# Two cached-attention decode steps on one core: groups of four heads with all their rows, 4 MB loads, and one loop of five equal rounds

## The chip, the cores and the metric

The kernel runs on one core of a Trainium2 chip. The metric is the device time of one execution in microseconds. Next to it stands the span of a profiled execution, from its first to its last instruction, mostly 1.4 to 1.6 us shorter than its time. A ratio is the mean time of one kernel's fast runs over the mean of the other's fast runs of the same rounds, so it is not quite the ratio of the medians that are quoted. A difference within 2% counts as "the same".

## The reference

Two independent decode steps, A and B, with the same shapes: one query token, 32 query heads, 16 key/value heads of 128, a cache of 8192 rows. A looks only at the last 2048 rows, B at all of them.

```python
# x [1,1,576], k_cache, v_cache [1,16,8192,128], wq [576,4096], wo [4096,576], all bf16
W = min(4096, max(256, Sk // 4))                      # 2048, for A
q = (x @ wq).reshape(B, Sq, 32, 128).transpose(0, 2, 1, 3)
k = jnp.repeat(k_cache[:, :, Sk - W:, :], 2, axis=1)  # A; B takes all rows
v = jnp.repeat(v_cache[:, :, Sk - W:, :], 2, axis=1)
p = softmax(einsum("bhqd,bhkd->bhqk", q, k) * Dh ** -0.5)
o = einsum("bhqk,bhkd->bhqd", p, v)
out = o.transpose(0, 2, 1, 3).reshape(B, Sq, 4096) @ wo   # [A's 576, B's 576]
```

Every byte is used once: 84 MB of K and V, 9.4 MB of wq, 9.4 MB of wo. This is a job of loading, and the arithmetic has to keep up.

## The kernel before

A small scheduler records operations and works out the semaphore waits; the large ones are emitted in hardware loops. PE (TensorE) transposes K, ACT (ScalarE) and DVE (VectorE) evict the transposes, PE makes scores, ACT the exponentials, PE multiplies with V. Loads are of 2 MB: a slot holds, in each partition, one run of 64 rows of one head, 16 KB.

```python
    def load_kv(arrs, g, s, slots, name, after=()):
        P = 0 if g == 0 else 1
        i = s if g == 0 else 4 * ((g - 1) % 2) + s
        ch = 128 // G[P] * TS                        # G = [4, 2] heads a slot, TS = 64 rows a partition
        r0 = base[P] + (0 if g == 0 else (g - 1) // 2 * ch)
        def src():
            return arrs[P][0, i * G[P]:(i + 1) * G[P], r0:r0 + ch, :].rearrange("g (p t) d -> p g (t d)", t=TS)
        load(slots[:, s, :], src, [(name, s)], "%s%d" % (name, s), after)

    K_ON = lambda g: g < 5
    V_OF = {1: 0, 3: 1, 4: 2, 5: 3, 6: 4}            # in which round each group's V is used
    # [cut: q, transposes, scores, softmax]
    for g in range(7):
        if g < 5:
            for s in range(NS):
                load_kv(ks, g, s, kslots, "k", ...)
        if g in V_OF:
            for s in range(NS):
                load_kv(vs, V_OF[g], s, vslots, "v")
        # [cut: transposes and scores of group g; every second round the softmax of two groups]
        if g == 6:
            weights(0)
            weights(1)
            combine(0)                               # A's heads, ready for wo
        if g in V_OF:
            for s in range(NS):
                v_slot(V_OF[g], s, 20 + s, g)        # 64 matmuls of 128 columns a slot
            v_keep(V_OF[g])                          # DVE: mask and sum of opsum, 2 x 0.69 us
```

K runs ahead of V: the last twelve K and V loads are all V. At the end comes wo, 32 heads of each step, four matmuls of 144 columns a head; B's share is loaded in pieces of 14, 8, 4, 3, 2 and 1 heads.

```python
    combine(1)                                       # B's heads: DVE scales, PE sums, DVE copies
    for P in range(2):
        for Q, lo, n, view, res, after in wo_loads:
            if Q == P:
                wo_part(P, lo, n, view, res)
        finish_out(P)
```

## Time and profile before

The time is 248.36 us (median of 4 runs, 248.31 to 248.45).

| what | before |
|---|---|
| span of the profile | 247.2 us |
| load queue's packets, share of 16 engines | 98.3% |
| bytes read | 102.76 MB |
| PE busy | 69% |
| first to last load packet (from the trace's packet records) | 1.02 to 244.35 us |
| from the last load packet to the end of the span | 2.8 us |

The page of the kernel before: the span, busy time of PE with its share, the DMA row (busy tenths in 40 equal slices), GB/s in those slices, and the load queue with packets, MB and share.

```profile
span 247.2 us, 7504 instructions
...
PE 169.9 (69%) x3406; PEld 132.4 (54%) x3406; DVE 80.9 (33%) x152; ACT 87.2 (35%) x92; POOL 12.9 (5%) x49
...
DMA  8999999999999999999999999999999999999993
GB/s 316 382 446 420 436 424 424 427 427 435 427 426 424 424 432 422 426 424 427 430 432 430 430 424 438 424 427 424 430 427 432 427 432 430 432 425 423 422 410 143
...
q1 hardware_dynamic: 7936, 102.77, 98.3%
```

The load queue never rests. The busy share of PE is an average and does not show a bound here: PE idles 31% of the span while the queue is busy throughout.

The end of the chain of waits (start, duration, what), before:

```profile
220.41 23.98 DMA vslots<-in_B_wo_dram
244.40 0.04 issue
244.44 0.71 PE ktps L654 x10
...
245.18 0.31 DVE outsb L660
```

The chain waits 24 us for B's wo; only ten matmuls and a copy come after it. PE's own timeline there (start, duration, what, in brackets the idle time before it and what ended it):

```profile
222.70 1.08 PE L565 MATMUL opsum<-vslots,ptm 128*32 128x128 bf16 x64 [1.81 <-PEq L214]
226.65 1.92 PE L638 MATMUL misc<-acc,pick 128*128 128x32 f32 x8 [2.87 <-DVE acc L632]
228.49 1.87 PE L654 MATMUL ktps<-kslots,opj 128*32 128x144 bf16 x56
232.25 2.35 PE L654 MATMUL ktps<-kslots,opj 128*32 128x144 bf16 x72 [1.88 <-DMA kslots<-in_A_wo_dram]
238.49 1.87 PE L654 MATMUL ktps<-kslots,opj 128*32 128x144 bf16 x56 [3.89 <-DMA kslots<-in_B_wo_dram]
241.29 1.15 PE L654 MATMUL ktps<-vslots,opj 128*32 128x144 bf16 x32 [0.93 <-DMA vslots<-in_B_wo_dram]
...
244.44 0.68 PE L654 MATMUL ktps<-vslots,opj 128*32 128x144 bf16 x12 [0.15 <-DMA vslots<-in_B_wo_dram]
```

L565 is the last V slot, L638 B's combine, L654 wo. V and combine are done at 228.5, and from there PE follows its loads: nearly every group of wo waits for a DMA.

### The profile page before, as it was taken

To read this page: it belongs to the slowest core of one execution; us is meant where nothing else is said; L and a number is where in the kernel's file an instruction comes from. 1 tells how busy PE (TensorE), PEld (TensorE's weight loads), DVE (VectorE), ACT (ScalarE), POOL (GpSimd) and SP (SyncE) were. 2 spreads that over 40 slices of the span, in tenths; PEclk is the share of its full clock that TensorE was granted. 3 is DMA by queue.
4 is the path that set the end of the run, shared out by engine and by line. 5 is a ranking of instruction groups with operands and counts; after the bars stand their busy time and mean duration, and the time that the engine had idled before them with its cause. 6 is when DMAs were issued, how large, how long until landed. Compare 5 with 4: busy or idle time off the path is not lost. (4 is left out here: it accounts for less than half of the span.)

```text
span 247.2 us, 7504 instructions
## 1 busy us (share of the span) xinstructions
PE 169.9 (69%) x3406; PEld 132.4 (54%) x3406; DVE 80.9 (33%) x152; ACT 87.2 (35%) x92; POOL 12.9 (5%) x49
## 2 busy tenths in 40 slices
PE   0083689993999479995999628998356344574634
PEld 0041286863786368864878428776244243474522
DVE  0010145463755026554555122556005004204000
ACT  2000057757587017776478104775300000000000
POOL 7501000000000000000000000000000000000000
PEclk9999779997999959999799965999957555578555
DMA  8999999999999999999999999999999999999993
GB/s 316 382 446 420 436 424 424 427 427 435 427 426 424 424 432 422 426 424 427 430 432 430 430 424 438 424 427 424 430 427 432 427 432 430 432 425 423 422 410 143
DMA packets 8235, 102.92 MB, mean 416 GB/s; under 512 B 1184, under 2 KB 1312, under 8 KB 2080
## 3 DMA queue, kind: packets, MB, share of 16 engines
q1 hardware_dynamic: 7936, 102.77, 98.3%
q8 instruction: 8, 0.13, 0.2%
q10 hardware_dynamic: 288, 0.00, 0.1%
q14 instruction: 3, 0.02, 0.0%
HBM read 102.76 MB, written 0.00 MB: 416 GB/s over the span
## 5 line engine op out<-in xcount | busy, mean ns | idle before, releaser
L480 ACT ACTIVATE kt<-ktps 128x1024 bf16<-128x1024 bf16 x80 | 78.0, 1021 | 52.9 <-PE ktps L474 52.9
L474 PEld LDWEIGHTS ktps<-ident,kslots 128*128 128x128 bf16 x1280 | 79.3, 104 | 26.2 <-issue 26.2
L474 PE MATMUL ktps<-ident,kslots 128*128 128x128 bf16 x1280 | 85.6, 230 | 10.7 <-PEq L214 10.7
L483 DVE COPY kt<-ktps 128x1024 bf16<-128x1024 bf16 x80 | 55.2, 691 | 52.8 <-PE ktps L474 52.7
L565 PE MATMUL opsum<-vslots,ptm 128*32 128x128 bf16 x1280 | 27.8, 261 | 26.8 <-PEq L214 22.7
L565 PEld LDWEIGHTS opsum<-vslots,ptm 128*32 128x32 bf16 x1280 | 25.0, 119 | 30.8 <-issue 30.7
L494 PE MATMUL sacc<-kt,qst 128*32 128x512 bf16 x320 | 25.7, 392 | 2.1 <-PEq L214 1.9
L574 DVE TENSOR_TENSOR diag<-opsum,rows 128x512 f32<-128x512 f32 x5 | 3.5, 692 | 54.8 <-PE opsum L565 54.8
L433 PE MATMUL opsum<-vslots,xpad 128*32 128x512 bf16 x64 | 8.1, 487 | 17.2 <-DVE xpad L418 12.7
L607 ACT ACTIVATE stat<-stat 128x1 f32<-128x1 f32 (+1 forms) x2 | 0.6, 294 | 36.7 <-DVE stat L605 36.7
L433 PEld LDWEIGHTS opsum<-vslots,xpad 128*32 128x32 bf16 x64 | 2.2, 117 | 20.0 <-issue 13.7
L465 POOL COPY qst<-qtm 128x64 bf16<-128x64 bf16 x20 | 4.5, 236 | 123.1 <-PE sacc L494 114.5
L654 PE MATMUL ktps<-kslots,opj 128*32 128x144 bf16 x184 | 6.1, 325 | 5.8 <-DMA kslots<-in_B_wo_dram 3.9
L439 ACT ACTIVATE qrow<-opsum 128x512 bf16<-128x512 f32 x2 | 1.2, 597 | 24.9 <-PE misc L433 24.9
L494 PEld LDWEIGHTS sacc<-kt,qst 128*32 128x32 bf16 x320 | 5.2, 94 | 8.7 <-issue 4.8
L531 ACT ACTIVATE psb<-sacc,stat 128x2048 bf16<-128x2048 f32 x3 | 5.9, 1967 | 8.5 <-DVE stat L525 8.5
L654 PEld LDWEIGHTS ktps<-kslots,opj 128*32 128x32 bf16 x184 | 5.2, 145 | 6.4 <-DMA kslots<-in_B_wo_dram 4.2
L433 PE MATMUL misc<-vslots,xpad 128*32 128x512 bf16 x64 | 7.9, 475 | 0.0
L441 DVE CAST qrow<-misc 128x512 bf16<-128x512 f32 x2 | 1.4, 692 | 15.9 <-PE misc L433 15.9
L638 PE MATMUL misc<-acc,pick 128*128 128x32 f32 x16 | 3.8, 404 | 3.6 <-DVE acc L632 2.9
L660 DVE CAST outsb<-ktps 128x144 bf16<-128x144 f32 x2 | 0.6, 308 | 16.1 <-PE ktps L654 16.1
L638 PEld LDWEIGHTS misc<-acc,pick 128*128 128x128 f32 x16 | 3.6, 328 | 3.8 <-DVE acc L632 3.0
(66 smaller groups left out, 62.1 us busy)
## 6 DMA issues: line engine op xcount, KB each, us to landing
kslots<-in_B_k_cache_dram SPq DMA_DIRECT2D x16, 2048.0 KB, 20.1
vslots<-in_B_v_cache_dram SPq DMA_DIRECT2D x16, 2048.0 KB, 18.5
kslots<-in_A_k_cache_dram SPq DMA_DIRECT2D x4, 2048.0 KB, 30.4
vslots<-in_A_v_cache_dram SPq DMA_DIRECT2D x4, 2048.0 KB, 24.1
vslots<-in_A_wq_dram SPq DMA_DIRECT2D x2, 2048.0 KB, 9.9
vslots<-in_B_wq_dram SPq DMA_DIRECT2D x2, 2048.0 KB, 20.3
kslots<-in_A_wo_dram SPq DMA_DIRECT2D x2, 2016.0 KB, 23.8
kslots<-in_B_wo_dram SPq DMA_DIRECT2D x1, 2016.0 KB, 31.2
```

Of the source, the lines that this page charges most:

```text
L433: ins = pe.matmul(qps[c][32 * j:32 * j + 32, :], lhsT=xpad[:, P, x, :], rhs=src[:, o:o + 512], start=(u == 0), stop=(u == WQ_UNITS - 1))
L441: add("dve", lambda dve: dve.tensor_copy(qrow[:, 512:1024], misc[:, :]), reads=[B_M], writes=[("qrow", 1)])
L465: add("pool", lambda pool: pool.tensor_copy(qst[:, s * 64:(s + 1) * 64], qtm[:, o:o + 64]), reads=[("qtm", KIND[g])], writes=[("qst", s)], ...
L474: ins = pe.matmul(ktps_bf[q][:, t * 128:(t + 1) * 128], lhsT=kslots[:, s, o:o + 128], rhs=ident[:, :], start=True, stop=True, is_transpose ...
L480: add("act", lambda act, q=q, dst=dst: act.activation(dst, ktps_bf[q], ACT.Copy), reads=[("bank", q)], writes=[("kt", u % NKT, q)], tag="e ...
L483: add("dve", lambda dve, q=q, dst=dst: dve.tensor_copy(dst, ktps_bf[q]), reads=[("bank", q)], writes=[("kt", u % NKT, q)], tag="e%d%d" % ( ...
L494: ins = pe.matmul(sacc[32 * j:32 * j + 32, 512 * half:512 * half + 512], lhsT=qst[:, s * 64 + e * 32:s * 64 + e * 32 + 32], rhs=rhs, start ...
L531: return act.activation(psb[:, :].rearrange("p (x g) -> p x g", g=2), src, ACT.Exp, bias=st(P, C_NB + k), scale=SCALE, accum_out=st(P, C_L ...
L565: ins = pe.matmul(opsum[32 * j:32 * j + 32, s * DH:(s + 1) * DH], lhsT=ptm[:, o:o + 32], rhs=vslots[:, s, b * 128:(b + 1) * 128], start=(u ...
L574: return dve.tensor_tensor(diag[:, g % 2, :, :], opsum[:, :].rearrange("p (s d) -> p d s", s=NS), m, ALU.mult)
L638: ins = pe.matmul(misc[:, 0:32], lhsT=pick[:, r, :], rhs=acc[:, d, 32 * r:32 * r + 32], start=(r == 0), stop=(r == 3))
L654: ins = pe.matmul(ktps[P][32 * j:32 * j + 32, 0:OUTW], lhsT=opj[:, P, jj:jj + 32], rhs=view[:, o:o + OUTW], start=(jj == 0), stop=(jj == H ...
```

## The change

The intent is longer runs and a simpler loop. Four heads with all 8192 rows make a group, so each partition of a B load holds 128 rows of one head, 32 KB, and a load is 4 MB. A's 2048 rows give 8 KB runs, in loads of 1 MB. A group's scores fit one bank without masking, V is multiplied 512 columns at a time, and every round does the same: K, softmax, V.

```diff
-SLOT = 8192
+SLOT = 16384
 ...
+            if g:
+                i = 4 * (g - 1) + 2 * s
+                return sp.dma_start(dst, arrs[1][0, i:i + 2, :, :].rearrange("e (p t) d -> p e (t d)", t=128))
+            for m in range(4):
+                i = 4 * m + 2 * s
+                src = arrs[0][0, i:i + 2, SK - W_A:, :].rearrange("e (p t) d -> p e (t d)", t=32)
+                ins = sp.dma_start(dst[:, m * UNIT:(m + 1) * UNIT], src)
 ...  [cut: scores of eight heads in one bank, no zeroing, no mask]
-                        ins = pe.matmul(opsum[32 * j:32 * j + 32, s * DH:(s + 1) * DH], lhsT=ptm[:, o:o + 32],
-                                        rhs=vslots[:, s, b * 128:(b + 1) * 128],
+                    ins = pe.matmul(opsum[32 * j:32 * j + 32, s * 512:(s + 1) * 512], lhsT=ptm[:, o:o + 32],
+                                    rhs=v[:, :, b:b + 128], start=(tt == 0), stop=(tt == 7), skip_group_check=True)
 ...
+            m = bass.AP(tensor=maskV, offset=0, ap=[[8, 128], [1, 8], [0, DH]])
+            return dve.tensor_tensor(diag[:, :, :], opsum[:, :].rearrange("p (y d) -> p y d", y=8), m, ALU.mult)
 ...
+    for g in range(NG):                    # five equal rounds
+        for s in range(2):
+            load_kv(ks, g, s, koff(s), KS[s], "k")
+        for s in range(2):
+            load_kv(vs, g, s, voff(s), VS[s], "v")
 ...  [cut: transposes, scores]
+        softmax_exp(g)
+        softmax_transpose(g, 18)
+        if g == NG - 1:
+            weights(g)
+            combine(0, (g, 18.6, LAST))
+        v_slot(g, 0, 20)
+        v_slot(g, 1, 21)
+        v_keep(g)
 ...  wq: one load of 36 KB rows for each step, in place of three of 16, 16 and 4 KB
+        (0, 0, 32, 0, [("k", 0), ("k", 1, 0)]),          # wo: step, first head, heads, place
+        (1, 0, 24, WQ_W, [("k", 1, 1)]),
+        (1, 24, 5, 2 * SLOT, [("v", 0, 0), ("v", 0, 1)]),
+        (1, 29, 2, 2 * SLOT + 5 * DM, [("w", 0)]),
+        (1, 31, 1, 2 * SLOT + 7 * DM, [("w", 1)])]
     combine(1)
     for P in range(2):
         [both wo parts, as before]
```

## The prediction

> **What bounds the kernel now.** The DMA queue, from start to end. The page shows DMA at 9 tenths or more in 38 of 40 slices and the load queue at 98.3% of 16 engines. It moves 102.76 MB, 424 to 432 GB/s in the middle (GB/s row). No compute engine exceeds 69%. The chain of waits ends in 24.0 us of DMA (B's wo), then 0.71 us of PE, a copy and the output store. So only four things move the time: the stream's rate, holes in it, its start, and what follows its last byte.
>
> **Rate.** The trace's DMA packets are one per row of a load: 16384 B takes 611 ns at best, 4096 B 159 ns. That is 8.3 ns fixed plus bytes at 27.2 B/ns, or 435 GB/s over 16 engines: the ceiling that the Trainium skill gives (DMA: Bandwidth & Descriptors, "Where 436 GB/s comes from"); the trace agrees. Estimates from this fit, if a longer row stays one packet: 8 KB 310 ns, 32 KB 1214, 36 KB 1365. Per engine: B's K and V 156.4 -> 155.4 us, A's 39.1 -> 39.6, wq 22.1 -> 21.8, wo 22.5 -> 22.0, fewer completions -0.1. Sum about -1.3 us, all on the critical path.
>
> **Holes in the steady part.** None expected. A round brings 16 MB, about 39 us. Its PE work, by the timeline: 8 units of transposes and scores at 2.5 us warm (3 to 3.6 cold), 20 to 28 us; softmax and transpose about 4; V 4 to 7. K's first slot is free about 11 us after landing, while 20 us of loads are queued behind it. V in 512-column matmuls streams the same columns (1280x128 = 320x512); it saves weight loads. Score zeroing, the mask and two-group chunks go too. All off the path.
>
> **Start.** The x loads share the engines: in the trace each alternates one 10 B x packet with one 16 KB row, as the Trainium skill says (same page, "Queues, rings and completion order": round-robin at packet granularity). x A landed at 11.5 us, x B at 13.7. With 36 KB rows each turn costs 1.36 us: I estimate x A at 16 to 19 us, x B near 25. B's q matmuls then end near 31 to 32 us (before 29.4). They gate A's second K load; the first K load runs out near 33 us. An issue takes about 1 us to its first packet: a hole of 0 to 2 us, expected 0.5.
>
> **End.** wo B's first piece grows from 14 heads to 24. The 14 took 1.87 us of PE, 0.118 us a head at the granted 0.5 clock; 24 take 2.8, then 8 more 0.95, against 2.9 us for the remaining small loads. PE finishes some 0.4 us later after the last byte than before.
>
> **Sum.** 248.4 - 1.3 + 0.5 + 0.4 = **248.0 us**, range 246.3 to 250.0. Faster by over 2%: 0.03. Within 2%: 0.92. Slower: 0.05.
>
> **What would show it.** 32 KB packets near 1214 ns, 8 KB near 310; mean GB/s up by at most 2. In the DMA queue's own waits, the one for the q matmuls ends at 31 to 32 us, and the DMA slice around 32 to 36 us is lower. x lands late. PE runs without a break over its last 128 matmuls. PE's busy share falls.
>
> **What would make it wrong.** Rows over 16 KB split into several packets: no rate gain, but no late x. A larger stride between the engines' addresses slowing HBM reads. A fixed cost at load boundaries that I missed. A starting hole of 3 us or more. Coarser slots starving the queue in a cold-clock round.

## The result

The changed kernel takes 249.76 us (249.68 to 250.01, 4 runs) against 248.36: ratio 1.0058, 95% interval 1.0043 to 1.0072. The median is inside the predicted range (one run, 250.01, is just outside) and inside 2%, but 1.4 us slower where 0.4 faster was expected.

| what | before | after |
|---|---|---|
| time | 248.36 us | 249.76 us |
| span of the profile | 247.17 us | 248.39 us |
| first to last load packet | 1.02 to 244.35 | 1.01 to 242.71 |
| from the last load packet to the end | 2.82 us | 5.69 us |
| packets of K and V, median | 16 KB: 0.614 us | 32 KB: 1.218 us; 8 KB: 0.312 us |

The spans differ by 1.22 us, and this splits, to 0.01 us: the loads end 1.64 us earlier, and what follows them is 2.87 us longer. The page after, the same lines:

```profile
span 248.4 us, 5439 instructions
...
PE 165.4 (67%) x2428; PEld 117.5 (47%) x2428; DVE 87.3 (35%) x140; ACT 87.3 (35%) x95; POOL 10.7 (4%) x48
...
DMA  9998999999999999999999999999999999999980
GB/s 350 410 463 372 421 423 421 420 421 420 446 449 438 433 423 427 422 422 443 434 433 438 433 427 427 427 433 433 433 438 443 422 427 433 422 454 411 433 334 9
...
q1 hardware_dynamic: 5632, 102.77, 97.0%
```

The last slice shows it: the DMA row ends in 0 and the rate in 9 GB/s, where before it was 3 and 143. The loads are done and the kernel is not. (Single slices swing by 20 to 40 GB/s because a packet is counted whole; the 8 KB stretch from slice 5 to 10 at 420 and the 32 KB stretch after it are the readings.) The end of the chain of waits after:

```profile
232.24 1.24 DVE diag L548
233.48 0.02 issue
233.50 1.87 DVE acc L384
235.37 0.79 DVE accs L599 x4
236.16 0.04 issue
236.21 1.19 PE misc L612 x29
237.40 3.40 PE ktps L627 x105
240.80 1.21 issue
242.01 2.18 PE ktps L627 x127
244.19 1.65 issue
245.84 0.55 PE ktps L627 x21
```

No DMA stands in it any more. V ends, DVE keeps its result (1.24 + 1.87 us), scales it, PE combines it (L612), and only then come all 256 wo matmuls (L627) in one row, A's 128 as well. PE's timeline:

```profile
225.85 6.33 PE L540 MATMUL opsum<-slots,ptm 128*32 128x512 bf16 x64
236.21 1.19 PE L612 MATMUL misc<-accs,pickB 128*32 128x32 f32 x29 [4.02 <-DVE accs L599]
...
237.37 3.43 PE L627 MATMUL ktps<-slots,opj 128*32 128x144 bf16 x102
242.01 2.18 PE L627 MATMUL ktps<-slots,opj 128*32 128x144 bf16 x127 [1.21 <-issue]
245.84 0.54 PE L627 MATMUL ktps<-slots,opj 128*32 128x144 bf16 x21 [1.65 <-issue]
```

PE idles 4.02 us for the keep although A's heads were ready at 226.2 and A's wo had landed (its last packet ended at 231.6). B's first 24 heads were in at 239.9 and PE reached B's part only at about 242.4, 20 matmuls after its first pause. Twice PE stops with "issue": nothing that the profile shows held it.

### The profile page after: what moved, and what is told of

Same layout as the page of the kernel before. It is cut to its first block, busy times and chain, and to the rows that moved or that the text cites. A ratio compares the mean times of both kernels' runs of the same rounds, so it can differ in the third digit from the quotient of the medians.

```text
span 248.4 us, 5439 instructions
## 1 busy us (share of the span) xinstructions
PE 165.4 (67%) x2428; PEld 117.5 (47%) x2428; DVE 87.3 (35%) x140; ACT 87.3 (35%) x95; POOL 10.7 (4%) x48
## 5 line engine op out<-in xcount | busy, mean ns | idle before, releaser
L466 PE MATMUL ktps<-ident,slots 128*128 128x128 bf16 x1280 | 87.7, 234 | 32.2 <-PEq L214 30.0
L466 PEld LDWEIGHTS ktps<-ident,slots 128*128 128x128 bf16 x1280 | 81.7, 106 | 47.6 <-issue 47.6
L540 PE MATMUL opsum<-slots,ptm 128*32 128x512 bf16 x320 | 28.7, 537 | 4.2 <-PEq L214 4.2
L425 PE MATMUL opsum<-slots,xpad 128*32 128x512 bf16 x144 | 11.2, 482 | 19.0 <-DVE xpad L413 19.0
L540 PEld LDWEIGHTS opsum<-slots,ptm 128*32 128x32 bf16 x320 | 11.6, 129 | 20.0 <-issue 17.9
L548 DVE TENSOR_TENSOR diag<-opsum,maskV 128x1024 f32<-128x1024 f32 x5 | 6.1, 1225 | 29.3 <-PE opsum L540 29.3
L508 ACT ACTIVATE psb<-sacc,stat 128x1024 bf16<-128x1024 f32 x5 | 5.6, 1114 | 11.9 <-DVE stat L502 11.9
L384 DVE TENSOR_REDUCE acc<-diag 128x128 f32<-128x1024 f32 x5 | 9.4, 1871 | 0.2
L627 PE MATMUL ktps<-slots,opj 128*32 128x144 bf16 x256 | 6.4, 268 | 2.9 <-issue 2.9
L627 PEld LDWEIGHTS ktps<-slots,opj 128*32 128x32 bf16 x256 | 5.7, 118 | 3.3 <-issue 3.3
```

Of the source, the lines that this page charges most:

```text
L384: add("dve", lambda dve: dve.tensor_reduce(out, view, AX.X, ALU.add), reads=reads, writes=writes, tag=tag)
L425: ins = pe.matmul(opsum[32 * j:32 * j + 32, c * 512:(c + 1) * 512], lhsT=xpad[:, P, x, :], rhs=slots[:, o:o + 512], start=(u == 0), stop=( ...
L466: ins = pe.matmul(ktps_bf[q][:, t * 128:(t + 1) * 128], lhsT=slots[:, o:o + 128], rhs=ident[:, :], start=True, stop=True, is_transpose=True)
L508: return act.activation(psb[:, :].rearrange("p (x g) -> p x g", g=2), src, ACT.Exp, bias=st(C_NB + g), scale=SCALE, accum_out=st(C_L + g))
L540: ins = pe.matmul(opsum[32 * j:32 * j + 32, s * 512:(s + 1) * 512], lhsT=ptm[:, o:o + 32], rhs=v[:, :, b:b + 128], start=(tt == 0), stop=( ...
L548: return dve.tensor_tensor(diag[:, :, :], opsum[:, :].rearrange("p (y d) -> p y d", y=8), m, ALU.mult)
```

## The experiments

Theories. **C**, order: ready work (A's wo) stands behind B's combine in PE's program, so PE's backlog, not a load, ends the kernel. **F**, instruction refills: the two "issue" pauses are PE running out of instructions. They are 127 matmuls apart, 254 to 256 instructions with the weight loads, and in the trace's packet records two 16 KB packets of the instruction queue start at 239.6 and 243.2, about a microsecond before each pause. The Trainium skill (Runtime: NRT & Kernel Launch, "Instruction fetch mechanics") says that instructions are refilled in 16 KiB blocks of 256. The rivals: **D**, the pauses are waits for wo data that are not named; **S**, my prediction's term, the 24-head piece alone sets the tail. **X** is my prediction's start term: late x delays B's q, which gates A's second K load. Every kernel below gave correct results.

They ran on three chips, each with the kernel before beside them (medians 248.36, 248.34 and 248.47 us). A trace is of one execution: those of e4 and e11 are the fastest of their six, those of e3 and e7 the slowest, e9's the second slowest.

Positions are counted as matmul records since the end of V, where B's combine counts 32 (16 float32 matmuls with two records each). After the change the first pause comes at 32 + 108 = 140 and the second 127 later, at 267.

### e1_pad84 and e6_pad_late: useless matmuls move the pauses

```diff
+    def pads(pe):
+        for _ in range(84):
+            ins = pe.matmul(misc[0:32, 0:1], lhsT=ident[:, 0:32], rhs=ident[:, 0:1], start=True, stop=True)
+        return ins
+    add("pe", pads, reads=["ident"], writes=[B_M])     # e1: before q; e6: after the loop, into sacc
```

> The changed kernel with 84 useless one-column matmuls at PE's start, done while PE waits for x. Theory F: the two pauses marked 'issue' in the last matmuls (1.21 us after 108 wo matmuls, 1.65 us after 127 more) are refills of PE's instructions, 128 matmul pairs apart in program order. Then the pauses move 84 matmuls earlier, to about wo matmul 24 and 151; the first falls mostly into PE's wait for the keep and costs little, the second stays, so 1.0 to 1.6 us faster than the changed kernel, 248.2 to 248.8 us. Rival D: the pauses are waits for wo data that the profile does not name: they stay after 108 and 235 matmuls, time unchanged at 249.8.

Measured: 249.25 us (247.89 to 250.82, 6 runs), ratio to before 1.0046 (1.0012 to 1.0080). One pause was left, of 1.76 us, after wo matmul 128 + 23 = 151, exactly 84 earlier. But the time scattered over 3 us: at the start PE's q matmuls ran later, and the loads ended 0.5 us later in the profiled run (243.21 us). F's first refill, which should have come at wo matmul 24, is not to be seen in this trace, neither as a pause nor as an instruction packet; why is open. So the pads went to another place:

> The changed kernel with the 84 useless matmuls put into PE's wait for the keep, after the loop, so that nothing before it moves (in e1 and e3 the same pads shifted the start too, and A's second K load came 1 to 2.5 us late). Theory F: one pause left, about wo matmul 151, of 1.2 to 1.8 us; 1.0 to 1.6 us faster than the changed kernel, 248.2 to 248.8, and no hole at 34 us. Rival D (waits for data): 249.8, pauses at 108 and 235.

Measured: 248.73 us (247.88 to 249.75, 6 runs), ratio 1.0014 (0.9993 to 1.0036). PE's timeline of e6:

```profile
231.03 2.24 PE L693 MATMUL sacc<-ident 128*32 128x1 bf16 x84
...
240.49 0.56 PE L627 MATMUL ktps<-slots,opj 128*32 128x144 bf16 x23 [0.55 <-DMA slots<-in_B_wo_dram]
242.56 2.69 PE L627 MATMUL ktps<-slots,opj 128*32 128x144 bf16 x105 [1.52 <-issue]
```

A's 128 wo matmuls run through; 23 of B's follow; then the pause. 84 + 32 + 151 = 267: the same position in PE's program. D falls, because the data did not move; F holds for where the pauses are. There is a second sign: in all 11 traces that have such pauses, e12's among them, PE went on 1.3 to 1.6 us after the end of a 16 KB packet of the instruction queue, in each of the 17 pauses. With eighty-four matmuls without a purpose the median is 1.0 us below the unpadded kernel's of the first call, and 0.8 below its second (e12), with ranges that overlap.

### e11_pad20: the control

> Control for e6: 20 pads in place of 84 at the same spot. Theory F: both pauses move 20 matmuls earlier, to about wo matmul 88 and 215, both still in PE's unbroken row: time as the changed kernel, within 0.5 us. If e6's gain came from pads keeping PE's clock up: part of the gain here too, with the pauses at 108 and 235.

Measured: 248.12 us (247.26 to 248.73, 6 runs), ratio 0.9988 (0.9974 to 1.0002), beside 249.54 for the unpadded kernel. The expectation of "unchanged" was wrong. PE's timeline of e11:

```profile
230.93 0.64 PE L693 MATMUL sacc<-ident 128*32 128x1 bf16 x20
235.12 0.80 PE L612 MATMUL misc<-accs,pickB 128*32 128x32 f32 x29 [3.55 <-DVE accs L599]
...
235.85 3.53 PE L627 MATMUL ktps<-slots,opj 128*32 128x144 bf16 x122
240.43 1.56 PE L627 MATMUL ktps<-slots,opj 128*32 128x144 bf16 x87 [1.04 <-DMA slots<-in_B_wo_dram]
242.76 0.85 PE L627 MATMUL ktps<-slots,opj 128*32 128x144 bf16 x41 [0.77 <-issue]
```

The second pause is at 20 + 32 + 128 + 87 = 267, as F says. The first is not to be seen: its packet started at 234.1, during PE's wait for the keep, where without pads it started at 238.9 to 239.6. So it seems that a few instructions put ahead of a wait got the refill going during the wait. The clock had a share as well, and the gain is not split: this trace is the fastest of the six runs, its combine took 0.80 us in place of 1.19, and A's 122 matmuls took 3.53 us (29 ns each) where unpadded 102 took 3.43 (34 ns each). The granted clock was full until 236.4 us here, and fell to 0.50 at 234.8 in the unpadded kernel.

### e2_woA_first: A's wo ahead of B's combine

```diff
-    combine(1)
     for P in range(2):
         for Q, lo, n, off, res in wo_loads:
             if Q == P:
                 wo_part(P, lo, n, off, res)
+        if P == 0:
+            combine(1)
         finish_out(P)
```

> The changed kernel with A's 128 wo matmuls and B's combine swapped on PE: they fill PE's 4 us wait for the keep. Theory C (program order puts 3.4 us of ready work last): if only order mattered 2.5 to 3.0 us faster, 246.9 to 247.3. With theory F beside it the pause after matmul 235 is still in B's last part and costs 1 to 1.6 us, so 247.6 to 248.9. Theory S (my prediction's: only B's 24-head piece sets the tail): unchanged, 249.8.

Measured: 247.79 us (247.55 to 248.07, 5 runs), ratio to before 0.9978 (0.9966 to 0.9991): 2.0 us faster than the changed kernel's first median, 1.75 than its second (e12). PE's timeline of e2:

```profile
232.13 2.18 PE L627 MATMUL ktps<-slots,opj 128*32 128x144 bf16 x128 [0.86 <-DMA slots<-in_A_wo_dram]
235.41 0.44 PE L612 MATMUL misc<-accs,pickB 128*32 128x32 f32 x11 [1.09 <-DVE accs L599]
238.59 0.91 PE L612 MATMUL misc<-accs,pickB 128*32 128x32 f32 x21 [2.73 <-issue]
240.35 3.98 PE L627 MATMUL ktps<-slots,opj 128*32 128x144 bf16 x128 [0.85 <-DMA slots<-in_B_wo_dram]
```

A's wo fills the wait for the keep. The first refill now stops the combine, at 128 + 11 = 139, but PE then still waits for a load, so it costs little; B's part runs through. From the last load packet (242.70) to the end are 3.64 us, in place of 5.69. C holds, and this kernel beats both, by 0.2% and 0.8%.

### e4_split and e5_first_split: the 24-head piece

```diff
-        (1, 0, 24, WQ_W, [("k", 1, 1)]),
+        (1, 0, 14, WQ_W, [("k", 1, 1)]),
+        (1, 14, 10, WQ_W + 14 * DM, [("w", 2)]),
```

> The changed kernel with wo B's first piece of 24 heads loaded as 14 and 10, as in the kernel before (14). Theory S: PE ends 0.4 us earlier, 249.3. F and C: PE is already behind (it reaches B's part at about 241, after the 24 heads landed at 239.9), so unchanged within 0.2 us, 249.7 to 249.9.

Measured: 249.22 us (248.07 to 250.20, 6 runs), ratio 1.0043 (1.0029 to 1.0057). The changed kernel's two measurements have 1.0058 and 1.0039, so no effect can be told from these; the expected 0.4 us of S is within the scatter too. The trace speaks for C: PE began B's part well after all 24 heads had landed, and paused at 108 and 235 as before.

> e2 (A's wo matmuls before B's combine) with wo B's first piece loaded as 14 and 10 heads. In e2 PE began B's part at 240.35 on the landing of 24 heads and ended 1.6 us after the last byte. Theory S as the second limit behind C: PE can start B's part when 14 heads have landed (236.4) and B's combine is done (239.5 in e2), so it ends 0.8 to 1.2 us earlier: span 245.2 to 245.6, time 246.7 to 247.1. If the tail is still set by refills or by clock alone: as e2, 247.8.

Measured: 247.74 us (247.47 to 248.22, 6 runs), ratio 0.9975 (0.9961 to 0.9989): e2's time. The expected 0.8 to 1.2 us did not come. The refill in the combine (2.08 us) held B's part until 239.8, and at the half clock its 128 matmuls took to 244.3, past the last packet at 243.1. So after C, the next limit is not the piece.

### e7_halves: a shorter keep

```diff
-        add("dve", go, reads=B_O + ["maskV"], writes=["diag"], tag="keep")
-        sums(acc[:, g, :], diag[:, :, :].rearrange("p y d -> p d y"), ["diag"], [("acc", g)])
+        for h in range(2):        # mask and sum of one V slot's bank each, the first under the second's matmuls
+            ...
+        add("dve", lambda dve: dve.tensor_tensor(acc[:, g, :], acc[:, g, :], accs[:, g, :], ALU.add), ...)
```

> The changed kernel with the keep (mask and sum of the V result, 3.1 us on DVE) done in two halves, the first under the second V slot's matmuls. If PE's end is a serial chain from the last K through softmax, V, keep, combine and wo (theory C in general), all after the keep comes 1.3 to 1.5 us earlier: 248.3 to 248.5. If the tail hangs on the landing of wo B (S or D): unchanged, 249.8.

Measured: 249.01 us (248.29 to 249.40, 6 runs), ratio 1.0017 (0.9999 to 1.0034). In the trace PE's wait for the keep shrank from 4.02 to 2.97 us; the time moved by 0.5 to 0.75 us, with ranges that overlap. The end of PE's timeline of e7 (L635 is wo there):

```profile
236.96 2.73 PE L635 MATMUL ktps<-slots,opj 128*32 128x144 bf16 x102
241.65 4.28 PE L635 MATMUL ktps<-slots,opj 128*32 128x144 bf16 x148 [1.96 <-issue]
```

The direction fits a serial chain, the size is not settled: the first pause grew to 1.96 us, and the second is missing, but the 148 matmuls after the first took 29 ns each, most of them at half clock, where the changed kernel's 127 took 17.

### e3_both and e8_both_wq16: the hole at the start

e3 is e2 with e1's 84 pads at the start.

> Both edits. F and C together: no pause after B's data has landed, the end is set by the last load again, 2.8 to 3.2 us after its last byte at 242.7: span 245.5 to 246.0, time 246.8 to 247.3, faster than both kernels. C alone: as e2. S: unchanged, 249.8.

Measured: 249.39 us (248.34 to 249.97, 6 runs), ratio 1.0035 (1.0019 to 1.0052). The tail did as hoped: no pause. But the loads ended 2 us later, because of a hole far ahead. Stretches of e3 (window, length, busy time with counts of PE, PEld, DVE, ACT, POOL, then granted clock, DMA share, GB/s):

```profile
30.00:32.00 2.00, 2.00 (x24) 0.87 (x20) 0.00 (x0) 0.00 (x0) 0.00 (x0) 0.50 1.02 430
32.00:34.00 2.00, 1.97 (x28) 0.70 (x20) 0.00 (x0) 0.00 (x0) 0.00 (x0) 0.77 0.91 369
34.00:36.00 2.00, 0.46 (x11) 0.43 (x12) 1.42 (x6) 0.60 (x1) 0.00 (x0) 1.00 0.42 102
```

The same stretch of the changed kernel:

```profile
34.00:36.00 2.00, 0.29 (x6) 0.32 (x7) 0.36 (x1) 0.00 (x0) 0.00 (x0) 1.00 1.01 422
```

This is the hole that the prediction feared, at the place it named. B's q matmuls must free the slot before A's second half of K can load. They ended at 31.5 us after the change and at 34.0 in e3, since they began 1.3 us later in e3 and took 6.96 us in place of 5.76. The granted clock was 0.50 until 32.9 us in e3. The Trainium skill (TensorE: Matmul & The Clock Gate, "What's actually happening") says that the gate knows only half and full rate; the clock records of these traces agree, with 0.5 and 1.0 alone. At the full rate the same 72 took 4.07 us (e2). So the changed kernel has no more than about half a microsecond to spare here: e1's ended at 32.1 and its loads ended 0.5 us later.

e8 is e3 with wq in 16, 16 and 4 KB rows:

```diff
-        load(slots[:, off:off + WQ_W], ..., res, "wq%d" % P)
-        q_part(P, off, res)
+        for c, lo, n in ((0, 0, 8192), (1, 8192, 8192), (2, 16384, 2048)):
+            load(slots[:, off + lo:off + lo + n], ..., "wq%d%d" % (P, c))
+        q_part(P, off, res + [("wqx", P, 1), ("wqx", P, 2)])
```

> e3 (84 pads at the start, A's wo first) with wq loaded in rows of 16, 16 and 4 KB in place of 36 KB. Theory X (my prediction's start term: x waits one wq row per turn, then B's q matmuls gate A's second K load): x A lands by about 12 us in place of 17, B's q matmuls end by 30 to 32 in place of 34, the hole of 2 us at 34 us goes, 1.5 to 2 us faster than e3, 247.4 to 247.9. If x is not what delays q (cold clock or refills alone): the hole stays, 249.4.

Measured: 248.70 us (248.55 to 249.19, 4 runs), 0.7 us below e3's median, with ranges that overlap. x's last packet came at 13.2 us in place of 24.7 to 26.0 in the kernels with 36 KB rows, so long rows do delay x. But B's q ended at 32.9, not by 32, and the hole shrank without closing (344 GB/s from 34 to 36 us, and the loads ended 0.8 us later than in the changed kernel), because B's q then waited for the last of its own wq, until 26.7. X is right about x, wrong about what x gates.

### e9_best and e10_best_16k: all together, and run length alone

e9 is e5 with 84 pads after the loop, ahead of A's wo. e10 is e9 with each of B's K and V loads cut into two of 16 KB runs:

```diff
-                return sp.dma_start(dst, arrs[1][0, i:i + 2, :, :].rearrange("e (p t) d -> p e (t d)", t=128))
+                op.also.append((32, sp.dma_start(dst[:, 0:SLOT // 2], src[:, :, 0:SLOT // 2])))
+                return sp.dma_start(dst[:, SLOT // 2:SLOT], src[:, :, SLOT // 2:SLOT])
```

> e5 (A's wo before B's combine, wo B as 14 and 10 heads) with the 84 useless matmuls after the loop, ahead of A's wo, so that the refill that stopped e5's combine for 2.1 us falls into A's wo and the next into B's first 23 matmuls. Theories F, C and S together: B's part starts near 237.5 in place of 239.8 and follows its loads; PE ends 0.8 to 1.0 us after the last byte in place of 1.3; span 245.3 to 245.8, time 246.8 to 247.3. If the cold clock, not the refill, holds B's part back: as e5, 247.7.

Measured: 248.82 us (248.21 to 250.26, 6 runs), ratio 1.0017 (0.9995 to 1.0040): slower than e5. PE's timeline of e9:

```profile
234.23 1.04 PE L627 MATMUL ktps<-slots,opj 128*32 128x144 bf16 x52
236.69 1.35 PE L627 MATMUL ktps<-slots,opj 128*32 128x144 bf16 x73 [1.43 <-issue]
237.83 0.88 PE L612 MATMUL misc<-accs,pickB 128*32 128x32 f32 x32
239.08 0.56 PE L627 MATMUL ktps<-slots,opj 128*32 128x144 bf16 x23 [0.38 <-DVE opj L615]
242.84 3.42 PE L627 MATMUL ktps<-slots,opj 128*32 128x144 bf16 x105 [3.20 <-issue]
```

The pauses are where F put them, after 84 + 55 = 139 and 128 later, inside A's wo and after B's first 23. Their cost was misjudged: the second lasted 3.20 us, on the path, since its packet started only at 240.2, after PE had run dry at 239.6; and the clock was at half from 241.7, so the last 105 matmuls took 3.42 us. F gives the place of a refill, not its moment.

> e9 with B's K and V loads cut into two loads of 16 KB runs each, as the kernel before has them. Packets of 16 KB at 0.611 to 0.618 us in place of 32 KB at 1.218: 256 per engine, 156.4 to 158.2 us in place of 155.9. If e9's end is set by the loads: 0.5 to 1.5 us slower than e9. If e9 is still bound by PE's chain behind the last K: 0.4 to 1.2 slower as well through K's landing; if large runs gain nothing: equal.

Measured: 249.74 us (248.65 to 250.25, 6 runs), ratio 1.0043 (1.0025 to 1.0061). The median is 0.9 us above e9's, with ranges that overlap. The loads themselves are clear: their last packet ended at 244.63 against 242.89. The packets of B's K and V account for most of it, with 157.4 us an engine in place of 155.9. So 16 KB runs, in twice as many loads, cost 1.7 us of the stream.

### e12_after_again: the changed kernel beside the last three

> The changed kernel itself on this chip: 249.5 to 250.1 if the first four runs (249.7 to 250.0) were typical. The variants of it scattered over 2 us where the kernel before stays within 1; if the clock granted in the tail makes that, this one scatters too, 248 to 250.5.

Measured: 249.54 us (248.35 to 249.94, 6 runs), ratio 1.0039 (1.0019 to 1.0059). It scatters over 1.6 us, the kernel before over 0.7 (248.17 to 248.83, 11 runs). That a kernel which ends on PE inherits the chances of PE's clock would explain this, but it is not shown: the mean clock of e12's runs does not follow their times (249.13 us at 0.827, 249.94 at 0.835; only the fastest, 248.35, also has the highest, 0.847).

## Why the prediction was right or wrong

- **What bounds the kernel: right for before, wrong for after.** Before, the chain ends on a load. After, it ends on PE, and the sum of four load terms no longer added up to the time.
- **Rate: right in mechanism, a little small.** 1.3 us predicted, 1.64 measured between the last packets. Predicted packets of 1214 and 310 ns were 1218 and 312 in the median. e10 gives back 1.74 us.
- **Holes in the steady part: right.** In the packet records of the changed kernel the 16 engines idle 0.2 us on average between 50 and 230 us, against 0.3 before.
- **Start: right in part.** B's q ended at 31.5 us (predicted 31 to 32), and x was late (24.7 us, predicted near 25). The hole was 0 in the profile of the changed kernel where 0.5 was put in the sum; e3 shows it at 2 us as soon as q is 2.5 us later. The dip predicted for 32 to 36 us is absent. e8 refutes that the late x alone decides it.
- **End: this is the step that failed.** "PE finishes some 0.4 us later after the last byte than before" came to 2.87 us. The estimate let PE stand idle until B's 24 heads landed. In fact PE came late: V's matmuls of the last round ran to 232.2, the keep took 3.1 us where it had taken 1.4, and A's 128 wo matmuls, about 4 us of ready work at the clock they had, stood behind B's combine. Moving them took back about 2 us (e2). "PE runs without a break over its last 128 matmuls" failed with it: it stopped for 1.65 us there, and for 1.21 before, for instruction refills.
- **The net.** -1.64 of loads + 2.87 of tail = +1.23 on a span that grew by 1.22. The expected gain was made and then given back after the loads had ended. That the time still fell inside 246.3 to 250.0 is owed to the width of that range: none of the risks that the prediction names lies at the end, so there it was luck.

What stays open: what sets the moment at which PE asks for its next block (e11 and e9 surprised in opposite directions; in e6, e9, e10 and e11 the second packet of the tail started 6.0 to 6.3 us after the first, wherever PE stood), and how much of the last microsecond in e2 and e5 is refill and how much the half clock.

## What to carry to other kernels

When loads bound a kernel, add up what the last engine still has to do after its last input becomes ready, in program order, and not only after the last byte: ready work that stands behind a wait counts as work after it. Straight-line code behind a loop has its own supply limit: here 128 matmuls with their weight loads arrived no faster than one block in about 3.5 us, so 256 of them in one row cannot be quick however fast the engine is; spread them over the waits for data. And a gain in the rate of the stream shows in the time only if the stream still ends the kernel.

## What the Trainium skill lacked or had wrong

- Runtime: NRT & Kernel Launch, "Instruction fetch mechanics", says that crossing a 16 KiB block is mostly hidden. Here it was hidden where PE was waiting anyway, or where the matmuls ran mostly at half clock (e2's last 128 in 3.98 us and e7's last 148 in 4.28 us, without a pause); else PE stopped in the tail for 1.21 and 1.65 us (after), 2.73 (e2, in the combine) and 3.20 (e9). The page's block of 256 instructions agrees: pauses 127 or 128 matmul and weight-load pairs apart in every run that showed two.
- No page gives the rate of refills. Where PE did not wait in between, the 16 KB packets of the instruction queue started 3.5 to 3.7 us apart (3.53 after, 3.68 in e1, 3.51 in e4, 3.55 in e7 and e12).
- DMA: Bandwidth & Descriptors, "Queues, rings and completion order", speaks of a packet as several descriptors. In these traces each row of a load is one packet, up to 36 KB, and the turn that another queue waits for grows with it: x's last packet ended at 13.3 us with 16 KB rows (before) and at 24.7 with 36 KB rows (after).
- The same page's table of measured bandwidth goes by the size of a transfer, and the page gives a cost per packet for small ones alone (in the table's note, about 10.5 ns). Here, at loads of 2 MB and more, the length of the run in a partition still counted: an estimated 8 ns a packet (from 4 KB in 159 ns and 16 KB in 611), 12 ns for each packet that e10 has more than e9 in B's K and V, and 1.7 us over 67 MB between 16 and 32 KB runs.
